# Fused RWKV recurrence and expert layer on one core: zero rows issued ahead of the loads, two copies moved, transposes in the last block, more zero matmuls

## The chip, the core and the metric

One NeuronCore of a Trainium2 chip runs the whole program. The metric is the device time of one execution in microseconds (us), the median of several executions. TensorE is written PE, its weight loads PEld, VectorE DVE, ScalarE ACT, GpSimd Pool; SP is the engine that issues most of the DMAs.

## What is computed

A linear recurrence over 4 batches, 8 heads, 768 tokens and a state of 48 x 48 per head, and then a layer with 8 experts, of which each token uses the one with the highest logit:

```python
for t in range(S):                      # attention part, y is (B, H, S, D)
    cur = np.einsum('bhd,bhe->bhde', u[None] * kt, vt)
    y[:, :, t] = np.einsum('bhd,bhde->bhe', rt, state + cur)
    state = wt[:, :, :, None] * state + np.einsum('bhd,bhe->bhde', kt, vt)
x = y.transpose(0, 2, 1, 3).reshape(B * S, H * D)          # 3072 tokens of 384
logits = x @ w_gate                                        # 8 experts
expert_idx = np.argmax(logits, axis=1)
for e in range(E):
    mask = expert_idx == e
    h = np.maximum(x[mask] @ w1[e], 0.0)                   # 384 -> 1024
    out[mask] = gate_w[mask, None] * (h @ w2[e])           # 1024 -> 384
```

## The kernel before

The recurrence is done in 24 blocks of 64 tokens (two batches to a block, `NB = 24`), one call of `iteration(n)` for each n from -3 to 23. The order of PE, DVE, ACT and Pool is written out by hand: each engine runs its instructions in the order of the Python text, and waits by semaphores for the others.

In `iteration(n)` PE transposes the keys of block n (`pe_kt`, line 474), multiplies by the carried state (`pe_inter`, 442), makes the 64 x 64 scores (`pe_a`, 430), then `pe_xc(n)`: transposes the finished rows of block n-1 (`pe_xT`, 497), makes the bonus coefficients of block n+2 (`pe_c`, 489) and runs some matmuls on zeros whose result nobody reads (`zeros`, 124; 16 of them while n < 4, else 6). Then come `pe_av` (451) and the state update `pe_dp` (463). All of `pe_xc`'s results share one PSUM bank, pool psM, which has one buffer: the next user of psM on PE waits until ACT has copied both the coefficients (`act_ct`, 394) and the transposed rows (`act_xT`, 421) out of it. The next user is, in three blocks of every four, the logits of the previous group of four blocks (`logit_mm` 503, `logit_tr` 510, `rank` 542), else the next block's `pe_xc`.

ACT copies kt out of PSUM (408), writes eight 64 x 64 diagonals of the next block (`act_diag`, 402), the state (`act_g`, 389), then xT, ct, and the finished rows xr (`act_xr`, 416). DVE blends the diagonals with the scores (`dve_at`, 354), which `pe_av` waits for, and does two scans, a reciprocal and a product for later blocks (332, 335, 341, 349). Pool multiplies r by the prefix (`pool_rh`, 376), r by k (`pool_rk`, 368, three blocks ahead; `pe_c` of a later block waits for it), and scatters finished rows by indirect DMA to xs, a table in HBM with 3072 rows per expert (`scatter`, 572), from block 7 on, one block's rows per iteration.

SP's queue issues, in order, the loads of block n+6 (`load`, lines 94 and 97, and `load_v`, 107) in iteration n, each when its buffer (six in a ring) is free. Rows 272 to 463 of each expert in xs are first filled with zero rows from the tile `zrow`, which Pool sets (`zero_rows`, 167, at the end of iteration 0). `prefill(e)` (313) issues the fill for expert e on SP's queue, for e = 0 to 7 at the end of iterations 1 to 8, behind that iteration's loads. Fills and scatters both write xs, so each is held until the ones before it in program order have landed.

From iteration 19 on the experts follow. `choose()` picks the first expert, its weights are loaded in four pieces (`load_piece`, 203 and 206), and `side()` splits one third of a piece into a high and a low part, on ACT (216) and DVE (218). `ua` is the first 256 rows of that expert; `halves(ua)` makes its gate weights (Pool copies gate and row number, 247; DVE adds and inverts, 249 and 250), and `transpose_rows` transposes them (PE 279, ACT 280, DVE 281) into PSUM banks `bk["t"]`. Before the change these banks exist only after `pctx.close()`, which is behind the last block. Then `mm1(ua, f)` (`expand`, 290 to 293) makes 128 of the 1024 hidden features at a time, for f = 0 to 7, between which the last two blocks' logits (`logit_few`, 519), `rank`, `place` and `scatter` stand. `sort_experts()` orders the other experts, SP reads that order into registers (`expert_of`, 651), and their weights are loaded from then on. `contract` (303) and the transposed form at 899 make the second product.

Of the kernel before, what the change touches and what calls it, by code (L numbers as in the profile page):

```python
# [53 lines left out]
def rwkv_moe_kernel(ctx, tc, rkw, vv, ub, wg, wr, w1, w2, out):  # L54
# [11 lines left out]
    psU = pctx.enter_context(tc.tile_pool(name="psU", bufs=1, space=PSUM))  # L66
    psA = pctx.enter_context(tc.tile_pool(name="psA", bufs=1, space=PSUM))
    psY = pctx.enter_context(tc.tile_pool(name="psY", bufs=1, space=PSUM))
    wk = mctx.enter_context(tc.tile_pool(name="wk", bufs=2))
# [59 lines left out]

    pre_ = []  # L130
# [9 lines left out]
    nc.vector.tensor_tensor(out=id2, in0=ident[:, 0:C], in1=ident[:, C:P], op=ALU.add)  # L140
    cmask = acon.tile([P, C], I32, name="cmask")
# [22 lines left out]
    zrow = wst.tile([P, ZJ * XC], F32, name="zrow", tag="wst")  # L164

    def zero_rows():
        nc.gpsimd.memset(zrow, 0.0)
        nc.gpsimd.iota(zrow.bitcast(I32).rearrange("p (j c) -> p j c", c=XC)[:, :, DM + 1], pattern=[[P, ZJ]], base=OOB,
                       channel_multiplier=1)

# [73 lines left out]
    def gate_weights(t):  # L244
        gi = gis.pop()
        p, nq = t.shape[0], t.shape[1]
        nc.gpsimd.tensor_copy(gi.bitcast(I32)[0:p, 0:nq], t.bitcast(I32)[:, :, DM:DM + 2])
        g = gi[0:p, 0:nq, 0:1]
        nc.vector.tensor_scalar(out=g, in0=g, scalar1=1e-9, scalar2=None, op0=ALU.add)
        nc.vector.reciprocal(g, g)  # L250
        return gi[0:p, 0:nq]
# [225 lines left out]
    def pe_xc(n):  # L477
# [3 lines left out]
        zeros(t[:, DM + H:], 16 if n < 4 else 6)  # L481
# [178 lines left out]
    def iteration(n):  # L660
        G, i = divmod(n, GRP)
        g = G - 1 if n >= 0 else -1
        whole = (g, 0, GRP)
        if n >= 0:
# [18 lines left out]
        if n == NB - 1:  # L683
            gate((NG - 1, 0, 2))
            side()
            side()
# [3 lines left out]
        act_diag(n + 1, range(4, 8))  # L690
# [8 lines left out]
        pe_xc(n)  # L699
        dve_pre(n + 2)  # L700
        act_xT(n - 1)
        act_ct(n + 2)
        pe_av(n)
        act_xr(n)
        act_pend(n + 2)
# [13 lines left out]
        if n == 0:  # L719
            zero_rows()  # L720
        if n == 1:
            late_constants()
        if 1 <= n < 9:
            prefill(n - 1)
# [45 lines left out]

    ET = mybir.EngineType
    with tc.manual_schedule(engines={ET.PE, ET.DVE, ET.Activation, ET.Pool}):
        last = NG - 1
        ka, kb = (last, 0, 2), (last, 2, 2)
        for n in range(-3, NB):
            iteration(n)
            if n == FIRST * GRP + 8:
                ua = rows_of(HA, 0, 0)
# [9 lines left out]
        scatter(last - 1, (1, 2, 3))  # L788
        t = psM.tile([P, BANK], F32, name="xc", tag="m")
        pe_xT(NB - 1, t)  # L790
        act_xT(NB - 1)
        pctx.close()
        psN = mctx.enter_context(tc.tile_pool(name="psN", bufs=1, space=PSUM))
        N = [psN.tile([P, BANK], F32, name=f"N{i}") for i in range(6)]
        bk["t"] = N[0:2]
        bk["b"] = [cell] + N[2:4]
        bk["c"] = N[4:6]
        pool_ids(last)
        scatter(last, (0, 1))
# [319 lines left out]
```

## Time and profile before

| | us |
|---|---|
| three executions | 441.26, 440.64, 438.7 |
| median | 440.64 |
| the profiled execution | 436.62 |
| its span, first to last instruction | 434.9 |
| PE busy | 387.4 (89%) |
| PEld busy | 357.4 (82%) |
| DVE busy | 260.1 (60%) |
| ACT busy | 208.8 (48%) |
| Pool busy | 133.2 (31%) |

The mean granted clock of PE over the span is 0.909 of full speed. In a timeline row, the number in brackets is how long the engine had been idle before the instruction, and what released it by the profile; "issue" and "remote" name no instruction of this core. PE's matmuls are pipelined, so the lengths of neighbouring rows overlap, and the start of the next row is the better measure. A wait for several things is put down to the one that came last by the profile, and where the named one had long been done, it was another, often a DMA.

### The profile page before, as it was taken

Reading aid. Unit: us, or ns where it says so; the run is one execution under the profiler, and the core shown is the slowest. Engines: PE = TensorE matmul, PEld = TensorE weight load, DVE = VectorE, ACT = ScalarE, POOL = GpSimd, SP = SyncE. Lnnn points to the kernel's source line nnn. Section 1 sums busy time; section 2 is a strip of 40 time slices with the busy share of each in tenths; the row PEclk is TensorE's granted clock in tenths of the full one; section 3 lists DMA queues with packets and bytes.
Section 4 is the critical chain, followed back from the end, with each engine's and each line's share of the span. In section 5 each row is a group of like instructions: output and inputs, shape, how many; then the busy total and the mean of one; then the engine's idle time right before and its main releaser. Section 6 shows DMA issues by size and latency. Waiting matters only on the chain.

```text
span 434.9 us, 13044 instructions
## 1 busy us (share of the span) xinstructions
PE 387.4 (89%) x5362; PEld 357.4 (82%) x5362; DVE 260.1 (60%) x447; ACT 208.8 (48%) x584; POOL 133.2 (31%) x171
## 2 busy tenths in 40 slices
PE   8879886699888796699889999999999999999890
PEld 6768665588767676599879999999999999999890
DVE  7546788844978764246665646647656577673310
ACT  1545764544667555325455545546456454551200
POOL 3753425573475723310201004004021072104031
PEclk9967999855999977559999999999999999999996
DMA  8996866646563722315955536556555567711001
GB/s 212 247 226 183 210 181 181 183 126 169 167 182 98 235 98 55 130 38 154 333 182 161 182 87 188 189 166 189 184 183 174 153 193 223 229 68 37 16 15 41
DMA packets 38214, 68.10 MB, mean 157 GB/s; under 512 B 8693, under 2 KB 20038, under 8 KB 38147
## 3 DMA queue, kind: packets, MB, share of 16 engines
q1 hardware_dynamic: 31026, 57.68, 46.0%
q0 software_dynamic: 7120, 9.51, 6.8%
q8 instruction: 44, 0.72, 0.7%
q14 instruction: 24, 0.19, 0.1%
HBM read 55.30 MB, written 12.04 MB: 155 GB/s over the span
## 4 chain that ended last, share of the span: by engine, by line
PE 49%; DMA 3%; DVE 2%; issue 1%; ACT 1%; SPq 1%; POOLq 0%; POOL 0%; ACTq 0%
PE N L290 12%; PE N L303 10%; PE N L899 6%; PE cell L290 6%; PE mM L290 5%; PE cell L899 3%; PE mM L899 3%; DMA wst<-in_w_dram 3%; PE N L279 2%; PE N L888 1%; SPq L651 1%; PE lt L519 1%; DVE hl L293 0%; DVE w2l L218 0%; DVE w1l L218 0%
## 5 line engine op out<-in xcount | busy, mean ns | idle before, releaser
L254 POOL DMA_INDIRECT out_dram<-ot,gi x16 | 22.3, 1392 | 103.4 <-issue 72.0
L402 ACT ACTIVATE at<-id,ct 128x64 f32<-128x64 f32 x192 | 50.4, 338 | 0.0
L354 DVE COPY_PREDICATED at<-cmask,ap 128x512 f32<-128x512 int32 x24 | 17.5, 729 | 42.8 <-ACT kt L408 39.0
L376 POOL TENSOR_TENSOR rh<-rkwt,pre 112x512 f32<-112x512 f32 x24 | 28.9, 1204 | 41.5 <-DVE pre L332 33.8
L254 POOL DMA_INDIRECT out_dram<-ort,gi x13 | 17.6, 1356 | 72.6 <-issue 23.6
L572 POOL DMA_INDIRECT xs<-xr,pi x24 | 25.6, 1068 | 44.2 <-issue 12.0
L218 DVE TENSOR_TENSOR w1l<-wst,w1h 128x512 fp32r<-128x512 f32 x48 | 32.9, 690 | 8.4 <-ACT w1h L216 8.2
L303 PE MATMUL N<-w2h,hh 128*126 128x384 f32 (+4 forms) x104 | 36.0, 346 | 1.4 <-ACT hh L292 1.4
L218 DVE TENSOR_TENSOR w2l<-wst,w2h 128x512 fp32r<-128x512 f32 x48 | 32.2, 689 | 6.2 <-ACT w2h L216 5.9
L303 PE MATMUL N<-w2h,hl 128*126 128x384 f32 (+4 forms) x104 | 35.1, 337 | 0.0
L368 POOL TENSOR_TENSOR rk<-rkwt 112x512 f32<-112x512 f32 x24 | 30.6, 1273 | 14.7 <-DMA rkwt<-in_rkw_dram 8.9
L303 PE MATMUL N<-w2l,hh 128*126 128x384 f32 (+4 forms) x104 | 35.0, 337 | 0.0
L293 DVE SCALAR_TENSOR_TENSOR hl<-N,hh 128x256 fp32r<-128x256 f32 (+8 forms) x37 | 19.4, 525 | 25.1 <-ACT hh L292 23.8
L216 ACT ACTIVATE w1h<-wst 128x512 fp32r<-128x512 f32 x48 | 29.6, 623 | 5.2 <-DMA wst<-in_w_dram 5.2
L341 DVE TENSOR_TENSOR_SCAN suf<-rkwt,cell 112x536 f32<-112x536 f32 x24 | 30.5, 1271 | 0.7
L332 DVE TENSOR_TENSOR_SCAN pre<-rkwt,cell 112x536 f32<-112x536 f32 x24 | 30.1, 1255 | 1.3 <-DMA rkwt<-in_rkw_dram 1.3
L216 ACT ACTIVATE w2h<-wst 128x512 fp32r<-128x512 f32 x48 | 28.8, 624 | 4.0 <-DMA wst<-in_w_dram 4.0
L451 PE MATMUL yp<-vt,at 64*64 64x48 f32 x768 | 21.5, 248 | 9.8 <-issue 5.0
L292 ACT ACTIVATE hh<-N 128x256 fp32r<-128x256 f32 (+8 forms) x37 | 17.2, 465 | 26.3 <-PE N L290 25.1
L408 ACT ACTIVATE kt<-ap 128x448 f32<-128x448 f32 x22 | 11.9, 542 | 37.3 <-PE ap L430 33.9
L290 PE MATMUL N<-xh,w1h 128*128 128x440 f32 (+6 forms) x84 | 28.8, 343 | 0.0
L290 PE MATMUL N<-xh,w1l 128*128 128x440 f32 (+6 forms) x84 | 28.6, 341 | 0.0
(182 smaller groups left out, 1027.8 us busy)
## 6 DMA issues: line engine op xcount, KB each, us to landing
wst<-in_w_dram SPq DMA_DIRECT2D x48, 256.0 KB
wst<-in_w_dram SPq DMA_DIRECT2D x16, 768.0 KB
rkwt<-in_rkw_dram SPq DMA_DIRECT2D x72, 96.0 KB
rkwt<-in_rkw_dram SPq DMA_DIRECT2D x24, 238.0 KB
vt<-in_vv_dram SPq DMA_DIRECT2D x24, 192.0 KB
wck_t<-in_wr_dram SPq DMA_DIRECT2D x6, 768.0 KB
rkwt<-in_rkw_dram SPq DMA_DIRECT2D x12, 224.0 KB
xs<-zrow SPq DMA_DIRECT2D x8, 289.5 KB
```

What stands on the lines that cost most here:

```text
L216: nc.scalar.activation(hi, st[:, cs], AF.Copy)
L218: nc.vector.tensor_tensor(out=lo, in0=st[:, cs], in1=hi.bitcast(F32), op=ALU.subtract)
L254: i = nc.gpsimd.indirect_dma_start(out=out[:, :], out_offset=bass.IndirectOffsetOnAxis(ap=t.bitcast(I32)[:, q, 1:2], axis=0), in_=rows, in ...
L290: nc.tensor.matmul(hp, a, x[p][:, j, :], start=(i == 0), stop=(i == 8))
L303: nc.tensor.matmul(op, a[:, cs], w2v(wt, w, f), start=(i == 0), stop=(i == 23))
L332: nc.vector.tensor_tensor_scan(out=d["pt"][:, 0, 0:NW], data0=d["w"], data1=cell[:RP, 0:1].broadcast_to([RP, NW]), initial=1.0, op0=ALU.mu ...
L341: nc.vector.tensor_tensor_scan(out=suf[:, ::-1], data0=d["w"][:, ::-1], data1=cell[:RP, 0:1].broadcast_to([RP, NW]), initial=1.0, op0=ALU. ...
L368: i = nc.gpsimd.tensor_tensor(out=d["rk"], in0=d["r"], in1=d["k"], op=ALU.mult)
L376: nc.gpsimd.tensor_tensor(out=d["rh"], in0=d["r"], in1=d["pre"][:, :, 1:C + 1], op=ALU.mult)
L402: nc.scalar.activation(d["at"][:, h // NQ, h % NQ, :], id2, AF.Copy, scale=d["ct"][:, h:h + 1])
L572: i = nc.gpsimd.indirect_dma_start(out=xsf, out_offset=bass.IndirectOffsetOnAxis(ap=ch["pi", G, b], axis=0), in_=xr[:, b, :], in_offset=No ...
L899: nc.tensor.matmul(pp, w, a, start=(i == 0), stop=(i == 23))
```

## The change

Five edits. (1) The pool with the recurrence's state, psU, gets its own context `uctx` on the right side of PSUM. In block 23 `open_n()` closes it, ahead of the pools of the scores and outputs, and opens two banks for the first rows' transposes; `halves(ua)` and the three calls of `transpose_rows` now stand inside iteration 23 (one of its two calls of `side()` gives way to them), and behind the last block `mm1(ua, 0)` comes ahead of `pe_xT(23)`, the scatters and the remaining logits, so that `mm1(ua, 3)` and no longer `mm1(ua, 2)` is the last ahead of `sort_experts()`. (2) `zero_rows()` runs on Pool during the setup, ahead of the mask, and the eight fills are issued at the head of iterations 0 to 5 (1, 1, 2, 1, 1 and 2 of them), ahead of that iteration's loads. (3) On ACT `act_ct(n+2)` and `act_xT(n-1)` come after four diagonals and the state, two more diagonals ahead of `act_xr(n)` and the last two behind it. (4) `pe_xc` runs 8 zero matmuls in place of 6 for n from 4 to 20, and 14 for n from 21 on. (5) In `gate_weights` DVE reads the gate from the loaded rows, and Pool copies only the row number; `tick()` places its transposes and splits at other points of the first expert's second product.

```diff
--- before.py
+++ after.py
@@ -63,9 +63,10 @@
     psC = mctx.enter_context(tc.tile_pool(name="psC", bufs=1, space=PSUM))
     psM = mctx.enter_context(tc.tile_pool(name="psM", bufs=1, space=PSUM))
     pctx = ExitStack()
-    psU = pctx.enter_context(tc.tile_pool(name="psU", bufs=1, space=PSUM))
     psA = pctx.enter_context(tc.tile_pool(name="psA", bufs=1, space=PSUM))
     psY = pctx.enter_context(tc.tile_pool(name="psY", bufs=1, space=PSUM))
+    uctx = ExitStack()
+    psU = uctx.enter_context(tc.tile_pool(name="psU", bufs=1, space=PSUM, side="right"))
     wk = mctx.enter_context(tc.tile_pool(name="wk", bufs=2))
     WKB = {"suf": 2, "kh": 4, "rh": 4, "rk": 4, "at": 3, "kt": 3, "oT": 2}
 
@@ -127,6 +128,13 @@
     zeros(wrm[:, 0:P], WARM[0])
     zeros(wrm, WARM[1])
 
+    zrow = wst.tile([P, ZJ * XC], F32, name="zrow", tag="wst")
+
+    def zero_rows():
+        nc.gpsimd.memset(zrow, 0.0)
+        nc.gpsimd.iota(zrow.bitcast(I32).rearrange("p (j c) -> p j c", c=XC)[:, :, DM + 1], pattern=[[P, ZJ]], base=OOB,
+                       channel_multiplier=1)
+
     pre_ = []
     for i in range(2):
         t = acon.tile([RP, 2, NW + SEG], F32, name=f"pre{i}")
@@ -138,6 +146,7 @@
     make_identity(nc, ident)
     id2 = const.tile([P, C], F32, name="id2")
     nc.vector.tensor_tensor(out=id2, in0=ident[:, 0:C], in1=ident[:, C:P], op=ALU.add)
+    zero_rows()
     cmask = acon.tile([P, C], I32, name="cmask")
     nc.gpsimd.memset(cmask, -1)
     for i in range(2):
@@ -161,13 +170,6 @@
     flag = const.tile([1, 1], I32, name="flag")
     none = const.tile([1, 1], F32, name="none")
     gis = [const.tile([P, 4, 2], F32, name=f"gi{e}") for e in range(E + 1)]
-    zrow = wst.tile([P, ZJ * XC], F32, name="zrow", tag="wst")
-
-    def zero_rows():
-        nc.gpsimd.memset(zrow, 0.0)
-        nc.gpsimd.iota(zrow.bitcast(I32).rearrange("p (j c) -> p j c", c=XC)[:, :, DM + 1], pattern=[[P, ZJ]], base=OOB,
-                       channel_multiplier=1)
-
     def late_constants():
         nc.gpsimd.memset(tri, 1.0)
         nc.gpsimd.affine_select(out=tri, in_=tri, pattern=[[1, P]], compare_op=ALU.is_gt,
@@ -244,9 +246,9 @@
     def gate_weights(t):
         gi = gis.pop()
         p, nq = t.shape[0], t.shape[1]
-        nc.gpsimd.tensor_copy(gi.bitcast(I32)[0:p, 0:nq], t.bitcast(I32)[:, :, DM:DM + 2])
+        nc.gpsimd.tensor_copy(gi.bitcast(I32)[0:p, 0:nq, 1:2], t.bitcast(I32)[:, :, DM + 1:DM + 2])
         g = gi[0:p, 0:nq, 0:1]
-        nc.vector.tensor_scalar(out=g, in0=g, scalar1=1e-9, scalar2=None, op0=ALU.add)
+        nc.vector.tensor_scalar(out=g, in0=t[:, :, DM:DM + 1], scalar1=1e-9, scalar2=None, op0=ALU.add)
         nc.vector.reciprocal(g, g)
         return gi[0:p, 0:nq]
 
@@ -478,7 +480,7 @@
         t = psM.tile([P, BANK], F32, name="xc", tag="m")
         pe_xT(n - 1, t)
         pe_c(n + 2, t)
-        zeros(t[:, DM + H:], 16 if n < 4 else 6)
+        zeros(t[:, DM + H:], 16 if n < 4 else 8 if n < NB - 3 else 14)
 
     def pe_c(n, t):
         if real(n):
@@ -661,6 +663,9 @@
         G, i = divmod(n, GRP)
         g = G - 1 if n >= 0 else -1
         whole = (g, 0, GRP)
+        if 0 <= n < 6:
+            for e in range(E * n // 6, E * (n + 1) // 6):
+                prefill(e)
         if n >= 0:
             load(n + 6)
             load_v(n + 6)
@@ -683,11 +688,11 @@
         if n == NB - 1:
             gate((NG - 1, 0, 2))
             side()
-            side()
+            open_n()
+            halves(ch["ua"])
         act_kt(n)
         act_diag(n + 1, range(0, 4))
         act_g(n + 1)
-        act_diag(n + 1, range(4, 8))
         dve_at(n)
         if full and i == 3:
             scatter(g, (0, 1) if g == FIRST else (0,))
@@ -697,11 +702,16 @@
             scatter(FIRST, (2, 3))
         pool_rk(n + 3)
         pe_xc(n)
+        if n == NB - 1:
+            for j in range(3):
+                transpose_rows(*(ch["ua"][k] for k in ("t", "nq", "rows", "x")), j)
         dve_pre(n + 2)
+        act_ct(n + 2)
         act_xT(n - 1)
-        act_ct(n + 2)
+        act_diag(n + 1, range(4, 6))
         pe_av(n)
         act_xr(n)
+        act_diag(n + 1, range(6, 8))
         act_pend(n + 2)
         act_pad(n + 4)
         if full and i == 2:
@@ -716,12 +726,8 @@
             t = rank(whole)
             if n == NB - 2:
                 logit_few((NG - 1, 0, 2), t)
-        if n == 0:
-            zero_rows()
         if n == 1:
             late_constants()
-        if 1 <= n < 9:
-            prefill(n - 1)
 
     todo = [(e, i) for e in range(E) for i in range(5) if i < 4 or 0 < e <= NWR]
     out_ = []
@@ -768,6 +774,11 @@
             halves(u)
         transpose_rows(u["t"], u["nq"], u["rows"], u["x"], j)
 
+    def open_n():
+        uctx.close()
+        psT = mctx.enter_context(tc.tile_pool(name="psT", bufs=1, space=PSUM, side="right"))
+        bk["t"] = [psT.tile([P, BANK], F32, name=f"N{i}") for i in range(2)]
+
     ET = mybir.EngineType
     with tc.manual_schedule(engines={ET.PE, ET.DVE, ET.Activation, ET.Pool}):
         last = NG - 1
@@ -775,7 +786,7 @@
         for n in range(-3, NB):
             iteration(n)
             if n == FIRST * GRP + 8:
-                ua = rows_of(HA, 0, 0)
+                ch["ua"] = rows_of(HA, 0, 0)
             if n == NB - 2:
                 for i in range(2):
                     side()
@@ -785,39 +796,38 @@
                 place(ka)
                 for i in range(2):
                     side()
-        scatter(last - 1, (1, 2, 3))
+        ua = ch["ua"]
+        pctx.close()
+        psN = mctx.enter_context(tc.tile_pool(name="psN", bufs=1, space=PSUM))
+        N = [psN.tile([P, BANK], F32, name=f"N{i}") for i in range(2, 6)]
+        bk["b"] = [cell] + N[0:2]
+        bk["c"] = N[2:4]
+
+        def mm1(u, f):
+            expand(wts[u["e"] % 2], f, u["x"], u["n"], u["hs"])
+
+        while sides and sides[0][2] < 2:
+            side()
+        mm1(ua, 0)
         t = psM.tile([P, BANK], F32, name="xc", tag="m")
         pe_xT(NB - 1, t)
         act_xT(NB - 1)
-        pctx.close()
-        psN = mctx.enter_context(tc.tile_pool(name="psN", bufs=1, space=PSUM))
-        N = [psN.tile([P, BANK], F32, name=f"N{i}") for i in range(6)]
-        bk["t"] = N[0:2]
-        bk["b"] = [cell] + N[2:4]
-        bk["c"] = N[4:6]
+        scatter(last - 1, (1, 2, 3))
         pool_ids(last)
         scatter(last, (0, 1))
-        for j in range(3):
-            trans(ua, j)
-
-        def mm1(u, f):
-            expand(wts[u["e"] % 2], f, u["x"], u["n"], u["hs"])
-
-        while sides and sides[0][2] < 2:
-            side()
-        mm1(ua, 0)
+        mm1(ua, 1)
         logit_few(kb)
         gate(kb)
-        mm1(ua, 1)
+        mm1(ua, 2)
         rank(kb)
         weigh(kb)
         place(kb)
         scatter(last, (2, 3))
-        mm1(ua, 2)
+        mm1(ua, 3)
         side(0)
         sort_experts()
         check_counts()
-        for f in range(3, 8):
+        for f in range(4, 8):
             mm1(ua, f)
             side(0)
         actx.close()
@@ -835,9 +845,10 @@
         tr = [(ub_, j) for j in range(3)]
 
         def tick():
-            if tr and nth["k"] % 2:
+            if tr and nth["k"] in ((1, 3, 4) if tr[0][0] is ub_ else (0, 2, 4)):
                 trans(*tr.pop(0))
-            side(nth["e"] + 1)
+            if nth["e"] or nth["k"] > 2:
+                side(nth["e"] + 1)
             nth["k"] += 1
 
         nth["k"] = nth["e"] = 0
```

## Rows read from the trace of the kernel before

**Rows 1.** The page: span, then TensorE's clock and the DMA engines in 40 slices.

```profile
span 434.9 us, 13044 instructions
...
PEclk9967999855999977559999999999999999999996
DMA  8996866646563722315955536556555567711001
```

**Rows 2.** Busy time: stretch, length, PE PEld DVE ACT Pool (instructions), clock, DMA share, GB/s.

```profile
41.70:64.60 22.90, 19.33 (x665) 16.16 (x661) 18.42 (x27) 15.35 (x60) 8.38 (x8) 1.00 0.71 191
64.60:84.30 19.70, 12.58 (x415) 10.22 (x412) 17.10 (x22) 11.80 (x45) 9.98 (x12) 0.96 0.63 171
84.30:105.10 20.80, 20.58 (x431) 17.54 (x431) 10.29 (x14) 9.02 (x33) 13.70 (x17) 0.50 0.52 149
...
177.20:195.40 18.20, 15.21 (x71) 14.53 (x72) 7.47 (x29) 5.31 (x14) 4.81 (x9) 0.50 0.12 45
195.40:223.10 27.70, 25.01 (x180) 24.07 (x179) 17.24 (x37) 14.37 (x33) 2.99 (x4) 1.00 0.74 233
223.10:424.40 201.30, 199.45 (x1155) 195.20 (x1155) 115.89 (x208) 92.53 (x183) 36.81 (x32) 1.00 0.48 146
```

**Rows 3.** Timeline of Pool, 57 to 90 us: start, length, what, idle before.

```profile
65.81 1.20 POOL L572 DMA_INDIRECT xs<-xr,pi  x1 [6.26 <-DMA rkwt<-in_rkw_dram]
...
73.60 1.44 POOL L572 DMA_INDIRECT xs<-xr,pi  x1 [4.12 <-DVE suf L341]
...
81.89 1.01 POOL L572 DMA_INDIRECT xs<-xr,pi  x1 [4.38 <-DVE at L354]
```

**Rows 4.** Timeline of SP's queue, 47 to 92 us: the zero rows.

```profile
60.13 0.48 SPq L313 DMA_DIRECT2D xs<-zrow  x1
...
69.67 0.48 SPq L313 DMA_DIRECT2D xs<-zrow  x1
...
77.95 0.48 SPq L313 DMA_DIRECT2D xs<-zrow  x1
```

**Rows 5.** Timeline of PE, 63 to 90 us.

```profile
84.28 1.03 PE L489 MATMUL xc<-ubt,rk 112*64 112x8 f32 x16 [3.19 <-POOL rk L368]
```

**Rows 6.** PE's waits, 41.7 to 155 us: total, times, longest.

```profile
PE xc L489 <- POOL rk L368: 4.7, 3, 3.2
...
PE lt L510 <- ACT ct L394: 2.1, 3, 0.7
...
PE rank L542 <- ACT ct L394: 1.4, 2, 0.7
PE lp L503 <- ACT ct L394: 1.4, 2, 0.7
```

**Rows 7.** Timeline of ACT in block 13.

```profile
109.31 1.05 ACT L402 ACTIVATE at<-id,ct 128x64 f32<-128x64 f32 x4
```

**Rows 8.** Timeline of PE, the zero matmuls of block 14.

```profile
114.34 0.49 PE L124 MATMUL xc<-wz,ones 128*128 128x120 bf16 x6
```

**Rows 9.** Timeline of PE, 160 to 172 us.

```profile
166.16 0.41 PE L542 MATMUL rank<-base,one 1*128 1x40 f32 x2 [1.38 <-ACT xT L421]
```

**Rows 10.** Timeline of PE, 168 to 196 us: the first rows' transposes.

```profile
177.92 1.06 PE L279 MATMUL N<-ident,xg 128*128 128x128 f32 x4
181.95 0.69 PE L279 MATMUL N<-ident,xg 128*128 128x128 f32 x2 [2.96 <-DVE x L281]
```

**Rows 11.** Timeline of ACT, 163 to 184 us.

```profile
175.14 0.49 ACT L421 ACTIVATE xT<-xc 128x384 f32<-128x384 f32 x1 [4.26 <-remote]
```

**Rows 12.** Timeline of DVE, 163 to 184 us.

```profile
181.20 0.17 DVE L249 TENSOR_SCALAR gi<-gi 128x2 f32<-128x2 f32 x1 [2.39 <-POOL gi L247]
```

**Rows 13.** Chain that ended last, 160 to 235 us: start, length, what.

```profile
207.19 10.23 DMA wst<-in_w_dram
```

**Rows 14.** Timeline of PE, 21 to 28 us.

```profile
25.68 0.99 PE L451 MATMUL yp<-vt,at 64*64 64x48 f32 x27 [2.54 <-issue]
```

**Rows 15.** Busy time by stretch, early.

```profile
20.00:26.00 6.00, 3.46 (x84) 2.84 (x86) 5.61 (x7) 3.47 (x13) 4.30 (x19) 0.89 1.06 240
```

More of the change, by code (lines that the diff above doesn't have):

```diff
@@ L787, in rwkv_moe_kernel @@
                     side()
-        scatter(last - 1, (1, 2, 3))
-        t = psM.tile([P, BANK], F32, name="xc", tag="m")
-        pe_xT(NB - 1, t)
-        act_xT(NB - 1)
+        ua = ch["ua"]
         pctx.close()
         psN = mctx.enter_context(tc.tile_pool(name="psN", bufs=1, space=PSUM))
-        N = [psN.tile([P, BANK], F32, name=f"N{i}") for i in range(6)]
-        bk["t"] = N[0:2]
-        bk["b"] = [cell] + N[2:4]
-        bk["c"] = N[4:6]
-        pool_ids(last)
-        scatter(last, (0, 1))
-        for j in range(3):
-            trans(ua, j)
+        N = [psN.tile([P, BANK], F32, name=f"N{i}") for i in range(2, 6)]
+        bk["b"] = [cell] + N[0:2]
+        bk["c"] = N[2:4]
         def mm1(u, f):
@@ L808, in rwkv_moe_kernel @@
         mm1(ua, 0)
+        t = psM.tile([P, BANK], F32, name="xc", tag="m")
+        pe_xT(NB - 1, t)
+        act_xT(NB - 1)
+        scatter(last - 1, (1, 2, 3))
+        pool_ids(last)
+        scatter(last, (0, 1))
+        mm1(ua, 1)
         logit_few(kb)
         gate(kb)
-        mm1(ua, 1)
+        mm1(ua, 2)
         rank(kb)
```

## The prediction

> **What bounds the kernel now.** First the page: the clock line shows TensorE below full speed in four places, at about 24 to 38, 82 to 106, 150 to 158 and 168 to 195 us [rows 1]. Then busy time by stretch [rows 2]. Behind 223.1 us PE is busy 199.45 of 201.3 us at clock 1.00 and the change touches nothing there: that part moves as a whole, and a gain ahead of it counts in full. Ahead of it the recurrence is uneven. The stretches begin at the first transposes of a block: blocks 4 to 7 take 22.9 us, 5.73 a block, with PE the busiest engine (19.33). Blocks 8 to 12, from 64.6 to 105.1 us, take 40.5 us, 8.1 a block, for the same work, and half of that runs at clock 0.50, the 1.2 GHz level.
>
> Why, Pool and SP's queue side by side show. Pool's first three scatters stand idle 6.26, 4.12 and 4.38 us [rows 3]. The profile names a load, a scan and a blend as releasers, but none of them is an input that comes due then. The times fit a ladder: a fill is issued at 60.13 us, the scatter behind it starts at 65.81; the fill of 69.67 comes 2.7 us after that scatter's row ended (65.81 + 1.20) and the next scatter follows at 73.60; the fill of 77.95, 2.9 us after that one's row (73.60 + 1.44), is followed by the scatter of 81.89 [rows 3, 4]. Fill and scatter both write xs, and each waits until the one before has landed, 3.9 to 5.7 us behind a fill. Pool is in order, so `pool_rk` stands behind each scatter, and PE waits 4.7 us for it in three places, the longest 3.19 us [rows 5, 6]. Behind that longest wait comes the half clock.
>
> **Edit 2, the fills first.** In program order all eight then stand ahead of every scatter, and the last two are issued at the head of iteration 5. The fill of 60.13 us is the one at the end of iteration 6, so that head is two blocks of 5.73 us sooner, at about 49 us; the first scatter's turn is at 65.81 - 6.26 = 59.6 us. Against 3.9 to 5.7 us of landing the wait is gone, and the two fills that queue behind scatters no longer hold up the loads behind them on SP. What is late next is PE itself. Five blocks at 5.73 us are 28.6 us against 40.5: **-11.9 us**. `zero_rows` on Pool moves to the setup, where PE, DVE and Pool wait for the first load anyway: nothing, and at most its own 1 us or so if that cover were gone. The fills now share the queue with the loads of blocks 6 to 11, each ahead of one: the loads run six blocks ahead, over 30 us, and eight fills of 290 KB at the 240 GB/s of [rows 15] are 1.2 us each. I take 0 for it; what it might cost is a rival.
>
> **Edit 3, ct and xT ahead of half the diagonals.** In seven blocks between 41.7 and 155 us PE waits 0.71 us at the user of psM behind `pe_dp`, 2.1 + 1.4 + 1.4 = 4.9 us in all, put down to ct, the last of the two copies [rows 6]. Four diagonals take 1.05 us on ACT [rows 7], and these move behind the copies: 0.71 goes wholly, and PE is late by its own work next. In blocks 8 to 12, four more such users, 2.8 us. Two diagonals stay ahead of `act_xr`, two go behind it: that copy too comes some 0.5 us sooner, and the late diagonals have most of a block before `dve_at` wants them. **Edit 4, more zeros.** Six take 0.49 us [rows 8], 0.08 each at most, so two more cost 0.16 us a block, 2.8 us over 17 blocks, if nothing hides them. So edits 3 and 4 together: between -4.9 us and nothing, since DVE is busy 18.42 us of the same 22.9 as PE [rows 2], and where a blend waits for DVE the freed time turns into a wait for it. I take **-3**.
>
> **Last blocks, 21 to 23.** Eight more zeros in each of three blocks are at 0.08 us 1.9 us. Against them stand block 21's wait of 0.71 and most of the 1.38 us that `rank` waits for xT in block 22 [rows 9], 1.05 of it by the diagonals. Sum: **+0.2**, between -1.8 (the zeros fill waits) and +1.
>
> **Edits 1 and 5, the transposes.** Now they stand between the last block and the first expert: from 177.92 us to the first product at about 182.6, 4.7 us, of which PE waits 2.96 [rows 10], because DVE waits 2.39 us for Pool's copy of the gates, which is behind scatters [rows 12]. In block 23 the six transposes take 1.06 + 0.69 us at the half clock, beside a wait of PE for DVE's blend; I count 0.3. Added: `mm1(ua, 0)` now wants the fifth split part of w1, which is made behind the last `rank`. A wait that the trace doesn't show; from about 1 us to as much as the 2.96 that it replaces; I take 1.5 below, since ACT is also copying there. Also one more product, `mm1(ua, 3)`, goes ahead of the sort. At 177.2 to 195.4 us, clock 0.50, PE ran 71 matmuls in 15.21 us busy [rows 2], 0.21 each, so nine are 1.9 us; `pe_xT(23)` only changes places with `mm1(ua, 0)`. -4.7 + 0.3 + 1.5 + 1.9 = **-1.0**, between -3.5 and +1.5.
>
> The sort matters because the second expert's weights are loaded by it, and the chain that ended last runs through 10.23 us of one such load [rows 13], with DMA at 0.74 of its engines' time in 195.4 to 223.1 us [rows 2]. An earlier end of PE's queue alone would be worth less.
>
> **Sum.** -11.9 - 3 + 0.2 - 1.0 = -15.7 us. The profiled execution took 436.62 us, span 434.9 and 1.7 around it, 4.0 less than the median of 440.64. I take the gain off the median: **424.9 us** (420.9 for an execution like the profiled one). With the terms' bounds added up (-4.9 to 0, -1.8 to +1, -3.5 to +1.5) it lies between 418.5 and 431.2, before the cases below.
>
> **Rivals.**
> *The clock holds into the experts.* The half clock from 168 us on follows idle stretches of PE in blocks 22 and 23: 1.38 us [rows 9], then more while ACT stands still 4.26 us with no releaser [rows 11]. With 14 zeros and the transposes in there the clock may stay at 2.4 GHz. Then 177.2 to 195.4 us with 15.21 us of matmuls gives back some 7 us, block 23 another 1: 417. For it speaks that the 1.38 us goes; against it, that nothing in the change removes the 4.26. Chance 0.30.
> *The early DMA traffic bites.* At 20 to 26 us the DMA engines are busy 1.06 of their time [rows 15], and there PE stands 2.54 us in the middle of one product, released by nothing shown [rows 14]; half clock follows [rows 1]. Eight fills in place of four by the head of iteration 5 lengthen the full stretch. One more such stop, 2.5 us, and two blocks at the half clock behind it: at 0.50, 431 matmuls took 20.8 us, 8.0 us for a block's 166, against 5.73 [rows 2]: 2.5 + 2 x 2.3 = 7 us, 432. Chance 0.15.
> The Trainium skill ("Runtime: NRT & Kernel Launch", section Instruction fetch mechanics) has each engine's instructions streamed over a DMA queue of their own, block by block, with the cost of crossing a block mostly hidden. If PE's stop is such a crossing, by that rule this rival would cost nothing and the forecast would stand; the 2.54 us row doesn't look hidden, and no row here shows that it is a fetch.
> *It doesn't do what it says.* If the scatters wait for the load that the profile names [rows 3] and not for a fill, the -11.9 stays away and 436.8 is left, faster by 0.9%. The ladder speaks against it. Chance 0.05.
> *Slower.* The DMA engines stay full until the fills are through, and PE stops in each of blocks 1 to 6 as in block 1: 2.5 + 2.3 us each, 29 us, against 15.7 gained: 454. It decides from 3.3 such blocks on (15.7 / 4.8). Against it: at 41.7 to 64.6 us, with four fills in it, the DMA share was 0.71 and the clock 1.00 [rows 2]. Chance 0.05.
>
> **Chances.** Forecast 0.45, own range 418.5 to 431; clock holds 0.30; one early stop 0.15; no effect of the fills 0.05; slower 0.05. The range reaches down to the held clock with half of the upside of the terms (414) and up to one early stop (433), and leaves out the last two cases and the far tails. About 0.5% (2.2 us) is what a measurement of this kernel can tell from no change. Faster by more than that: the forecast, the held clock, the early stop and most of the fourth case, 0.92; within it 0.04; slower 0.04.
>
> **What would show it.** Right: Pool's first scatter starts without a wait of several us, no PE wait for `pool_rk`, clock 1.00 from 41 to beyond 105 us, block 13 beginning near 90 us in place of 105.1; no 0.71 us waits for ct; all transposes of `ua` ahead of the last block's `pe_av`. Wrong: a scatter idle for 4 us still, half clock in blocks 3 to 8, DVE ending most of PE's waits, or a gap of over 2 us of PE ahead of `mm1(ua, 0)`. The sum would fail most easily at the tail, where the clock decides, and at blocks 4 to 20, if they run well below 5.73 us.

## Result, and the profile of the changed kernel

Beside the kernel before on one chip the changed kernel took **421.44 us** (median of 415.95, 420.69, 422.19 and 423.52) against 439.67 (436.52 to 441.26): a ratio of 0.955, 95% interval 0.944 to 0.967. The forecast was 424.9, range 414 to 433. Two repeats in later groups, told below, gave 418.3 against 435.8 and 418.1 against 430.2, the second with a ratio of 0.970 (0.963 to 0.977). So the changed kernel nearly keeps its time (418 to 421 us), and the kernel before moves: the gain is 12 to 18 us. The ratios here and below leave out executions more than 1.5% above the fastest of the same kernel, while medians and ranges hold them all.

The profiled execution is the slowest of the four: 423.52 us, its span 421.8, the mean granted clock 0.936. From its page, to be laid beside [rows 1]:

```profile
span 421.8 us, 13190 instructions
PE 383.2 (91%) x5419; PEld 353.2 (84%) x5420; DVE 257.0 (61%) x447; ACT 208.1 (49%) x584; POOL 133.7 (32%) x171
...
PEclk9997888998999595699999999999999999999996
DMA  8998855575662714128974456375466557801001
```

Of the half clock that [rows 1] show at 82 to 106 us a dip at 94 to 98 is left; the one at 30 to 36 us stands in both, and two are new, at 50 to 54 and 60 to 67 us. Busy time by stretch, as in [rows 2] (blocks 4 to 7, blocks 8 to 12, from `rank(ka)` on, the experts):

```profile
core 0: us, PE busy (x) PEld busy (x) DVE busy (x) ACT busy (x) POOL busy (x), PEclk, DMA share, GB/s
40.60:66.90 26.30, 23.43 (x674) 20.12 (x668) 19.15 (x28) 16.47 (x63) 11.73 (x12) 0.81 0.68 183
66.90:97.70 30.80, 27.15 (x854) 22.82 (x851) 24.14 (x34) 19.66 (x76) 19.21 (x23) 0.94 0.60 172
169.70:185.00 15.30, 15.21 (x103) 14.37 (x100) 8.42 (x30) 8.00 (x20) 4.66 (x8) 0.78 0.14 53
208.20:411.30 203.10, 199.76 (x1158) 195.26 (x1158) 117.40 (x210) 93.64 (x186) 37.83 (x33) 1.00 0.50 149
```

Blocks 8 to 12 take 30.8 us in place of 40.5, but blocks 4 to 7 take 26.3 in place of 22.9, at clock 0.81. The experts' stretch, begun here one matmul later than in [rows 2], takes 203.1 us in place of 201.3. Pool's first scatters, which stood 6.26, 4.12 and 4.38 us in [rows 3] (start, duration, idle before it and releaser):

```profile
62.17 1.20 POOL L574 DMA_INDIRECT xs<-xr,pi  x1 [3.39 <-DMA vt<-in_vv_dram]
...
67.47 1.01 POOL L574 DMA_INDIRECT xs<-xr,pi  x1 [0.16 <-ACT rkwt L382]
...
73.36 1.01 POOL L574 DMA_INDIRECT xs<-xr,pi  x1 [0.15 <-ACT ls L508]
```

The ladder is gone (the first still waits 3.39 us, at a half-clock block). PE's waits between 41 and 155 us, the view of [rows 6] (what waited, for what: us in all, times, longest):

```profile
PE ap L432 <- issue: 4.5, 7, 1.3
PE U L465 <- issue: 3.4, 3, 1.7
PE yp L453 <- DVE at L356: 1.3, 2, 0.9
PE yp L444 <- ACT xr L418: 1.0, 3, 0.4
```

No wait for rk (4.7 before) and 0.5 for ct (4.9 before). In their place stands "issue": time in which PE waited for nothing that the profile shows. What that is turned out to be the main question of the experiments.

### The profile page after: what moved, and what is told of

Same layout as the page of the kernel before. It is cut to its first block, busy times and chain, and to the rows that moved or that the text cites. A ratio compares the mean times of both kernels' runs of the same rounds, so it can differ in the third digit from the quotient of the medians.

```text
span 421.8 us, 13190 instructions
## 1 busy us (share of the span) xinstructions
PE 383.2 (91%) x5419; PEld 353.2 (84%) x5420; DVE 257.0 (61%) x447; ACT 208.1 (49%) x584; POOL 133.7 (32%) x171
## 4 chain that ended last, share of the span: by engine, by line
PE 73%; DVE 9%; issue 6%; DMA 4%; ACT 4%; another core or an unknown queue 1%; SPq 1%; POOLq 0%; POOL 0%; DVEq 0%; ACTq 0%
PE N L292 11%; PE N L305 10%; PE cell L292 6%; PE N L910 6%; PE mM L292 5%; PE yp L453 3%; PE xc L125 3%; PE cell L910 3%; DMA wst<-in_w_dram 3%; PE mM L910 3%; PE ap L432 3%; PE xc L491 2%; PE yp L444 2%; PE wrm L125 2%; PE U L465 2%
## 5 line engine op out<-in xcount | busy, mean ns | idle before, releaser
L256 POOL DMA_INDIRECT out_dram<-ot,gi x16 | 22.3, 1392 | 100.4 <-issue 72.0
L404 ACT ACTIVATE at<-id,ct 128x64 f32<-128x64 f32 x192 | 53.3, 343 | 0.0
L295 DVE SCALAR_TENSOR_TENSOR hl<-N,hh 128x256 fp32r<-128x256 f32 (+8 forms) x37 | 19.4, 524 | 24.1 <-ACT hh L294 22.8
L294 ACT ACTIVATE hh<-N 128x256 fp32r<-128x256 f32 (+8 forms) x37 | 17.2, 465 | 24.3 <-PE N L292 23.1
L410 ACT ACTIVATE kt<-ap 128x448 f32<-128x448 f32 x22 | 11.9, 543 | 34.9 <-PE ap L432 31.2
L292 PE MATMUL N<-xh,w1l 128*128 128x440 f32 (+6 forms) x84 | 28.6, 341 | 0.0
L292 PE MATMUL N<-xl,w1h 128*128 128x440 f32 (+6 forms) x84 | 28.6, 340 | 0.0
```

The lines of the kernel that those rows point to most:

```text
L256: i = nc.gpsimd.indirect_dma_start(out=out[:, :], out_offset=bass.IndirectOffsetOnAxis(ap=t.bitcast(I32)[:, q, 1:2], axis=0), in_=rows, in ...
L292: nc.tensor.matmul(hp, a, x[p][:, j, :], start=(i == 0), stop=(i == 8))
L404: nc.scalar.activation(d["at"][:, h // NQ, h % NQ, :], id2, AF.Copy, scale=d["ct"][:, h:h + 1])
```

## Experiments

Each kernel's diff is against the kernel named; " ..." marks lines left out. The kernels stood in three groups of four, each group on one chip beside the kernel before, whose medians there were 431.8 (the single edits), 435.8 (the four after that) and 430.2 us (the last four).

**The fills alone** (before, with edit 2).

```diff
+    zero_rows()
 ...
+        if 0 <= n < 6:
+            for e in range(E * n // 6, E * (n + 1) // 6):
+                prefill(e)
 ...
-        if n == 0:
-            zero_rows()
 ...
-        if 1 <= n < 9:
-            prefill(n - 1)
```

> The kernel before with edit 2 alone: zero rows set in the setup, eight fills at the head of iterations 0 to 5. Theory 1, each late fill holds the scatter behind it until it has landed and with it pool_rk and PE: 9 to 12 us faster (ratio 0.973 to 0.980), blocks 8 to 12 in 29 to 31 us in place of 40.5, no PE wait for pool_rk, scatters idle under 0.5 us from block 8 on. Theory 2, the stretch is slow for want of PE work at the blend (the copies, edit 3) and the fills only coincide with it: under 3 us faster, a scatter still idle for over 2 us. Theory 3, the early traffic costs PE stops in blocks 0 to 7: blocks 4 to 7 take 25 us or more in place of 22.9, as the profile of the changed kernel has it (26.3), and the gain is 6 to 9 us.

Measured: 427.5 us against 431.8, ratio 0.982 (0.971 to 0.993), so 4 us and not 9 to 12. Theory 1's mechanism is there (no PE wait for rk, the second to fourth scatter idle 0.16 us at most, blocks 8 to 12 in 31.9 us), and so is theory 3's loss: blocks 4 to 7 take 27.5 us, at clock 0.73. The gain is below what either theory gave.

**Copies and eight zeros alone** (before, with edit 3 and 8 zeros).

```diff
-        zeros(t[:, DM + H:], 16 if n < 4 else 6)
+        zeros(t[:, DM + H:], 16 if n < 4 else 8)
 ...
-        act_diag(n + 1, range(4, 8))
 ...
-        act_xT(n - 1)
         act_ct(n + 2)
+        act_xT(n - 1)
+        act_diag(n + 1, range(4, 6))
         pe_av(n)
         act_xr(n)
+        act_diag(n + 1, range(6, 8))
```

> The kernel before with edit 3 (ct and xT ahead of half the diagonals) and 8 zero matmuls in place of 6 from block 4 on, no other edit. Theory 1, the 0.71 us waits for ct go and DVE's blend takes part of it back: 3 us faster, between 0 and 4.9, PE waits for ct under 1 us in all in place of 4.9. Theory 2, the blend now waits for the two diagonals that moved: the waits move from ct to DVE's blend, time within 1 us of before. Theory 3, the two zeros lie in the open: 1 to 3 us slower.

Measured: 431.5 against 431.8, ratio 0.9995 (0.995 to 1.004): nothing. All PE waits for ct are gone between 41 and 155 us, yet the same view shows:

```profile
PE xc L489 <- POOL rk L368: 5.9, 3, 3.9
PE ap L430 <- issue: 5.9, 4, 3.6
PE U L463 <- issue: 3.5, 3, 1.9
PE yp L451 <- DVE at L354: 2.4, 3, 1.2
```

The blend did not take the time back (2.4 us, 3.0 before), as theory 2 wanted. In this profile the waits with no releaser did (11.1 us in the whole view, 4.0 before). That the edits call them forth isn't shown: 3.57 us of the 11.1 are one stop at 151.6 us, and the fills alone and the tail alone, without these edits, have its like (3.34 us at 148.2, 3.21 at 150.0).

**The tail alone** (before, with edits 1 and 5 and 14 zeros in blocks 21 to 23).

```diff
-        zeros(t[:, DM + H:], 16 if n < 4 else 6)
+        zeros(t[:, DM + H:], 16 if n < 4 else 6 if n < NB - 3 else 14)
 ...
-            side()
+            open_n()
+            halves(ch["ua"])
 ...
+        if n == NB - 1:
+            for j in range(3):
+                transpose_rows(*(ch["ua"][k] for k in ("t", "nq", "rows", "x")), j)
 ...
         mm1(ua, 0)
+        t = psM.tile([P, BANK], F32, name="xc", tag="m")
+        pe_xT(NB - 1, t)
+        act_xT(NB - 1)
+        scatter(last - 1, (1, 2, 3))
```

> The kernel before with edits 1 and 5 (the first rows transposed in block 23, gates without Pool's copy, mm1(ua, 0) ahead of the last copies) and 14 zero matmuls in blocks 21 to 23, fills and copies as before. Theory 1, a path shortened by the transposes, with the clock as it was: 1 us faster, between 3.5 faster and 1.5 slower; rank(ka) to the order's being ready 17 to 18.4 us. Theory 2, with the transposes out of the gap PE goes on without a stop and the clock returns earlier: 5 to 9 us faster, rank(ka) to the order ready in 13 to 14 us in place of 18.4, full clock from about 8 us behind rank(ka) on.

Measured: 427.3 us (421.6 to 432.0) against 431.8; the spread of its four executions leaves no interval. The trace is plainer. The 7 us behind `rank(ka)` by busy time, first of before, then of this kernel, and two of this kernel's PE rows:

```profile
176.00:183.00 7.00, 3.57 (x18) 3.03 (x18) 2.62 (x8) 3.19 (x8) 2.69 (x5) 0.50 0.25 94
```
```profile
172.50:179.50 7.00, 6.13 (x49) 5.55 (x49) 3.79 (x12) 3.60 (x11) 2.55 (x4) 1.00 0.33 128
```
```profile
175.25 0.39 PE L291 MATMUL cell<-x,w1l 128*128 128x256 f32 x1 [0.31 <-DVE w1l L219]
...
179.35 0.40 PE L543 MATMUL rank<-base,one 1*128 1x24 f32 x2
```

49 matmuls in place of 18, at 2.4 GHz in place of 1.2; `rank(kb)` starts 6.8 us behind `rank(ka)` (172.58) in place of 13.0. That is theory 2 by its mechanism; the 4.5 us of the medians lie just under the 5 to 9 that it gave.

**The changed kernel with late fills** (edit 2 undone).

> The changed kernel with edit 2 undone: zero rows and fills as before (iterations 0 and 1 to 8), all other edits in. Theory 1, the fills carry most of the gain: 8 to 12 us slower than the changed kernel, 429 to 433 us; scatters idle 4 to 6 us again in blocks 7 to 9, blocks 4 to 7 back to 23 us. Theory 2, the other edits carry it: within 4 us of the changed kernel's 421.4. If the edits' gains add up, this run and the one with the fills alone sum to the whole gain of 18 us.

Measured: 426.1 us against before's 431.8, ratio 0.985 (0.975 to 0.996). The changed kernel was not in this group; against its 418 to 421 us elsewhere it is 5 to 8 slower, between the two theories. Blocks 4 to 7 are back at 22.0 us, blocks 8 to 12 take 34.1. The 5.6 us won here and the 4.2 of the fills alone come to some 10 us, not to the 18 of the first comparison.

**The changed kernel again.**

> The changed kernel itself, beside the kernel before on the chip of the single edits' sort of clock. The edits measured one by one (fills alone 4.2 us, copies and 8 zeros 0.3, tail alone 4.5) add up to 9.0 us, against 18.2 in the first comparison. Theory 1, the edits add up, and the first comparison caught the kernel before on a chip where it ran slow: 2 to 2.5% faster than before here. Theory 2, they help one another (a wait taken out keeps the clock up for the next edit): 3.5 to 4.5% faster.

Measured: 418.3 us (410.8 to 423.4) against 435.8 (427.5 to 437.6). Before's seven executions here lie in two groups, at 427.5 to 428.6 and at 435.8 to 437.6, so 17.5 us is an upper end; the medians of its three short executions and of the changed kernel's two (410.8 and 416.9) lie 14 us apart, and theory 1 is not refuted. But this profile has one of the longest stops without a releaser, 3.34 us in the middle of one product, and the packet that goes with it (a PE row; then the line of the DMA queues for 142.9 to 143.0 us):

```profile
141.45 0.41 PE L432 MATMUL ap<-rh,kh 64*64 64x64 f32 x13
145.20 0.91 PE L432 MATMUL ap<-rh,kh 64*64 64x64 f32 x19 [3.34 <-issue]
```
```profile
q8 instruction: 1, 0.02, 58.5%
```

A packet of 0.02 MB on the instruction queue starts when PE has already stood for 1 us; by the packet's own times it lands at 143.86, and PE goes on 1.34 us behind that. Ahead of it SP's queue had asked for 2.3 MB of weights:

```profile
133.21 4.04 SPq L205 DMA_DIRECT2D wst<-in_w_dram  x6
137.44 0.39 SPq L208 DMA_DIRECT2D wst<-in_w_dram  x1
```

**The weight pieces one per block.**

```diff
-            feed()
+            feed(1)
+        if FIRST * GRP + 8 <= n < FIRST * GRP + 10:
+            feed(n - FIRST * GRP - 6)
 ...
-    def feed():
-        while len(out_) < 3:
+    def feed(most=3):
+        while len(out_) < most:
```

> The changed kernel with the first expert's first three weight pieces (768 KB each) asked for one per block, in blocks 19, 20 and 21, and not all three in block 19. In the profiles of before, of the changed kernel and of the four single edits PE stands, or its results come, 2 to 3.6 us late in block 20 or 21, about 1.3 us behind the landing of a 16 KB packet of the instruction queue that had started behind this load. Theory 1, PE's next instructions wait in the DMA engines behind bulk data: no stop of over 1.5 us in blocks 20 and 21, full clock there, 3 to 5 us faster than the changed kernel of the same call. Theory 2, the stop belongs to what PE, ACT or Pool do in these blocks: it stays at 2 to 3.6 us, time the same.

Measured: 414.6 us against the changed kernel's 418.3 in the same group, so 3.7 less, with ranges that overlap (408.4 to 418.4; 410.8 to 423.4). The stop of 3.34 us is now one of 1.49, and from 133 to 150 us the clock stands at half for 3.4 us only (PE; then the page's clock):

```profile
136.61 0.61 PE L453 MATMUL yp<-vt,at 64*64 64x48 f32 x19 [1.49 <-issue]
```
```profile
PEclk9959999999999898999999999999999999999996
```

The stop followed the load and not the block: theory 1, in this trace. The other profiles bear it out in part. Behind 133 us six of the ten with the pieces asked for at once have a stop of 2.7 to 3.6 us; of the four with spread pieces, those told below among them, none has one over 2.11, but each has one of 1.49 or more. Its 408.4 us is the shortest of the profiled executions.

**Six zeros** (the changed kernel, edit 4 undone: `zeros(..., 16 if n < 4 else 6)`).

> The changed kernel with edit 4 undone: 6 zero matmuls from block 4 on, also in blocks 21 to 23, and not 8 and 14. Theory 1, the zeros fill waits and cost nothing, and do nothing for the clock either: within 1 us of the changed kernel of the same call. Theory 2, they lie in the open: 2.8 + 1.9 us by the prediction's own prices, so 3 to 5 us faster than the changed kernel. Theory 3, they hold the clock: 2 to 5 us slower, half clock in more of the 40 slices between block 4 and the experts.

Measured: 415.5 us against 418.3, ranges overlapping (408.1 to 417.6). A gain of the size of theory 2 can't be told from chance here; see the second run of this kind below.

**All fills behind the setup's loads.**

```diff
-        if 0 <= n < 6:
-            for e in range(E * n // 6, E * (n + 1) // 6):
+        if n == -1:
+            for e in range(E):
                 prefill(e)
```

> The changed kernel with all eight fills issued right behind the loads of the setup, and not over the first six blocks. Theory 1, PE's stops with no releaser in blocks 2 to 7 of the changed kernel (1.95, 1.09 and 1.73 us) come from its instructions queueing behind fills and loads: stops of 30 to 60 us down to one at most, more of them before 30 us, blocks 4 to 7 near 23 us in place of 26.3, 2 to 4 us faster than the changed kernel of the same call. Theory 2, the loads alone make them: the same stops in blocks 2 to 7, time within 1 us. Theory 3, the loads of block 6 on come late behind the fills: a wait for a load at block 6 or 7, slower.

Measured: 414.7 us (414.5 to 423.0) against 418.3. Blocks 4 to 7 take 21.5 us, where the changed kernel took 28.3 in this group. Stops remain (1.31 us at 42 us, 0.74 at 50), three are now ahead of 32 us (2.43, 0.90 and 2.22), and no PE wait for a load shows. Theory 1 for the blocks; the count of stops is not what it said.

**Both together; the spread weights with late fills; both with six zeros; the changed kernel a third time.** The diffs are those above, put together.

> The changed kernel with both: the first expert's weight pieces asked for one per block, and all fills right behind the setup's loads. Theory 1, both take bulk data out of the way of PE's instructions and each keeps some of its gain: 408 to 413 us, 2 to 3% faster than the changed kernel of the same call, no stop of over 1.5 us behind 35 us. Theory 2, what is measured between kernels is chance in where PE happens to stop: within 3 us of the changed kernel of the same call, and stops of other lengths in other places.

> The changed kernel with the weight pieces one per block, and with edit 2 undone (fills at the ends of iterations 1 to 8, zero rows set at the end of iteration 0). It measures edit 2 without the long stop of blocks 20 and 21. Theory 1, waits for fills in blocks 7 to 9 cost what Pool and PE stand, but the prediction's 11.9 us was mostly a half clock that came with them by chance: 4 to 6 us slower than the same kernel with the fills in iterations 0 to 5 (414.6 us). Theory 2, the prediction's size: 10 to 12 us slower. Theory 3, early fills cost as much in blocks 1 to 7 as late ones in 7 to 9: within 2 us.

> The kernel with weight pieces one per block and fills behind the setup's loads, with 6 zero matmuls in place of 8 and 14. Theory 1, the zeros lie in waits: within 1.5 us of the same kernel with them. Theory 2, they cost their own time now that the stops are fewer: 2 to 4 us faster. Theory 3, they hold the clock: 2 to 5 us slower.

> The changed kernel, in the same call as the versions above and the kernel before, so that all stand on one chip. If the single edits add up: 2.5 to 3.5% faster than before; if the first comparison's size holds: 4 to 4.5%.

| kernel | median, us | range | ratio to before (430.2) |
|---|---|---|---|
| changed, third time | 418.1 | 413.6 to 423.4 | 0.970 (0.963 to 0.977) |
| spread weights, fills first | 416.5 | 406.8 to 420.0 | 0.954 (0.945 to 0.963) |
| the same, six zeros | 416.6 | 414.9 to 420.7 | 0.974 (0.968 to 0.980) |
| spread weights, fills late | 420.7 | 416.1 to 425.5 | 0.983 (0.977 to 0.989) |

The ratios and the medians order the kernels differently, and the second row's ratio rests on two executions (406.8 and 411.3). The changed kernel's third run is 2.8 to 3.0% faster than before, what its expectation has for edits that add up. The version with both beats it by 1.6 us in the median; whether that is real stays open. Its expected 408 to 413 was missed, and stops of 1.79 and 1.70 us remain behind 138 us. By the medians the zeros make no difference (416.6 and 416.5), theory 1, and late fills cost 4.2 us, theory 1 too, though measured against fills behind the setup's loads and not against the kernel that the expectation names. By the ratios late fills cost between 4 and 13 us. The kernel with late fills shows the price of the ladder without half-clock blocks ahead of it: blocks 4 to 7 run at clock 1.00 in 22.3 us, and then come the scatters, PE's waits and the busy time of blocks 8 to 12:

```profile
63.55 1.20 POOL L573 DMA_INDIRECT xs<-xr,pi  x1 [4.53 <-DMA rkwt<-in_rkw_dram]
...
71.17 1.01 POOL L573 DMA_INDIRECT xs<-xr,pi  x1 [3.94 <-DVE suf L342]
...
80.21 1.01 POOL L573 DMA_INDIRECT xs<-xr,pi  x1 [5.57 <-DVE pre L333]
```
```profile
PE xc L490 <- POOL rk L369: 6.2, 3, 4.6
```
```profile
64.30:99.70 35.40, 27.98 (x870) 23.58 (x865) 26.78 (x34) 20.32 (x75) 21.66 (x26) 0.86 0.60 179
```

35.4 us for blocks 8 to 12, against 29.0 at clock 1.00 with the fills first (the same view of that kernel):

```profile
44.50:66.20 21.70, 19.57 (x680) 16.56 (x676) 18.16 (x28) 15.43 (x59) 10.46 (x11) 1.00 0.58 168
66.20:95.20 29.00, 25.48 (x869) 21.38 (x862) 23.78 (x34) 19.69 (x74) 20.21 (x25) 1.00 0.65 197
```

The two lie 6.4 us apart, and PE's waits for rk are 6.2. PE is busy 2.5 us longer there (clock 0.86) and idle 3.9 us longer, so the waits for rk stand in part where the other kernel idles for other reasons. The ladder itself, which the prediction read from times of issue alone, shows here in the landings: the scatter of 63.55 us lands at 67.22 and the next fill is issued at 67.24; that of 71.17 lands at 75.41, and the next fill is issued at 75.42. Each waits for the one before.

## Why the forecast held, and which of its terms did not

Executions of one kernel differ by up to 13 us, so the terms are better read from all fourteen profiles by stage: the start of the first score product (`ap<-rh,kh`) of a block, and PE's last instruction. The a(n) below are those starts. Means, in us:

| | 0 to a(13) | a(4) to a(8) | a(8) to a(13) | a(13) to a(23) | a(23) to the end |
|---|---|---|---|---|---|
| late fills (5 profiles) | 102.6 | 23.1 | 36.2 | | |
| fills in iterations 0 to 5 (6) | 98.2 | 26.6 | 29.3 | | |
| fills behind the setup's loads (3) | 94.1 | 21.7 | 29.2 | | |
| copies as before (3) | | | | 63.1 | |
| copies moved, weights at once (7) | | | | 61.4 | |
| copies moved, weights spread (4) | | | | 59.1 | |
| tail as before (3) | | | | | 253.6 |
| new tail (11) | | | | | 247.6 |

The stages' differences add up to -4.4 - 1.7 - 6.0 = -12.1 us, what the last group measured (418.1 - 430.2). The forecast's terms were -11.9, -3, +0.2 and -1.0. Some of the prediction's own signs failed: half clock in blocks 4 to 7, which it had called a sign of being wrong, stood at 50 to 54 and 60 to 67 us; the first scatter still waited 3.39 us; block 13 began at 97.7 us and not near 90.

*Edit 2, -11.9.* The mechanism is right: the ladder of fills and scatters, the wait for rk behind it, and that PE is next (28.6 us forecast for blocks 8 to 12, 29.3 measured). The term is mis-sized at its other end and at its cover. 40.5 us was one profiled execution; five profiles with late fills take 33.4 to 40.7. The waits come to 6.2 us in the kernel with spread weights and late fills, and its stretch is 6.4 us longer. Half clock comes with them in blocks 8 to 12 of all five, for 10 to 14 us in four and for 23.9 in the one trace that the forecast used; with early fills it is 0 to 9 us. In the means the stretch shrinks by 36.2 - 29.3 = 6.9. And "I take 0 for it" on the queue was wrong: the early fills cost 26.6 - 23.1 = 3.5 us in blocks 4 to 7, which is the rival of the early traffic at half its price of 7. PE's stops of 0.5 us or more there are one to three in ten of these eleven profiles, of either kind. What differs is the clock behind them: five of the six profiles with fills in iterations 0 to 5 have 10 to 17 us of half clock in these blocks and take 26.3 us or more, and so does one of the five with late fills (6.8 us, 25.9); the other eight profiles have none and take 21.5 to 23.1. Net -4.4.

*Edits 3 and 4, -3.* The waits of 0.71 us went wholly, as forecast. At full clock something is left of it: blocks 4 to 7 take 23.1 us in before's profile, the only one of that kind with the old copies, and 21.5 to 23.1 us, in the mean 22.1, in the seven with the moved ones. But the edits alone gave 0.3 us, between 2.1 faster and 1.6 slower, and the -1.7 of the table lies within the spread of its profiles (62.4 to 64.1 with the old copies, 58.6 to 65.2 with the moved ones). What the forecast named as next (PE's own work, or DVE's blend) didn't take the rest; in the profile of the edits alone, stops with no releaser stand in its place, and why they do is open. The zeros, bounded at 2.8 us, cost nothing that two pairs of kernels can show.

*Tail, +0.2 and -1.0.* Mis-sized the other way: 6.0 us. Most steps are right one by one: the 2.96 us wait of [rows 10] is 0.6 to 0.9 us in ten of the eleven profiles (for the changed kernel's own see below); the new wait for the fifth split part is there, at 0.31 us behind 0.48 us for its ACT half with the tail alone; the six transposes stand in block 23. The step that failed is the clock, which the sum held at 0.50 and left to a rival with 0.30. In the three profiles with the old tail the half clock lasts until 17 to 20 us behind `rank(ka)` (the fourth dip of [rows 1] is one); in ten of the eleven with the new one it ends between 10 us ahead of and 7 us behind `rank(ka)`, in the eleventh 15 us behind. In the changed kernel's own profile it ends at 176.5 us, 6.8 behind, where before it ended at 195.4, 19.4 behind. So what stands ahead of the sort, the added product too, runs at twice the clock that the sum took. The zeros aren't needed for it: in the two kernels with six of them in blocks 21 to 23 the half clock ends 6.5 and 6.7 us behind `rank(ka)`.

A second step failed, "the change touches nothing there" of what lies behind 223.1 us. From one and the same matmul of the first expert's second product (at 223.95 us in before, 208.64 in the changed kernel) to PE's last one, the three profiles with the old tail take 200.4 to 200.5 us; of the eleven with the new one none takes less than 202.7, six take 202.7 to 202.9, and the mean is 203.6. So the new tail gains 9 us ahead of that point and loses 3 behind it. Two waits that before doesn't have stand there in all eleven (0.90 and 0.6 us), in the changed kernel:

```profile
214.67 0.50 PE L281 MATMUL N<-ident,xg 110*128 110x110 f32 x3 [0.90 <-DVE xl L283]
```
```profile
243.37 0.54 PE L899 MATMUL N<-ident,oT 128*110 128x128 f32 x3 [0.60 <-ACT oT L917]
```

They follow `tick()`'s new places for transposes and splits; no run has `tick()` changed by itself, so that it alone makes them isn't shown.

*The baseline.* 15.7 us were taken off 440.64, a median of three executions. Over the four groups before's median was 430.2 to 439.7 us, and over the three that hold the changed kernel the gain was 12.1 to 18.2. That the total came out near is in good part luck: the terms erred in both directions, and the start was taken from the group in which before was slowest. (The range's upper end of 433 is 1 us above what the early stop's own sum gives, 424.9 + 7.)

*Not explained.* In the changed kernel's block 23 ACT stands 5.86 us at the first copy of the transposed rows (161.30 to 167.16), as it stood 4.26 in [rows 11], and PE waits behind it:

```profile
168.06 0.69 PE L281 MATMUL N<-ident,xg 128*128 128x128 f32 x2 [3.33 <-DVE x L283]
```

PE's transposes begin at 163.66 us, so that copy comes 3.5 us behind them; in the other thirteen profiles, two of the same kernel among them, it comes 0.6 to 0.8 us behind. No instruction packet is near. It is left open. So is the price of the fills' traffic alone: a kernel without any fill wasn't tried, since it would read rows that nothing wrote.

## What to carry over

Price a wait by the wait and not by the length of the stretch that has it: the half clock that comes with it differs from execution to execution (10 to 24 us here), and further profiles show by how much. When a stall goes, look at what is queued in the DMA engines at that time, since PE's own instructions come through them; spread bulk loads or put them where PE has slack. A short PE gap at the border of two phases can be worth more than its length, when the clock stays down for what follows: here a wait of 2.96 us, and 6.0 us for the stage. And compare also the stretch that the change is taken to leave alone.

## What the runs showed of the hardware

By all that these traces show, PE's stops with no releaser are waits for its own instructions. The page of the changed kernel lists a queue of instructions (packets, MB, share of 16 engines):

```profile
q8 instruction: 44, 0.72, 0.8%
```

Each packet has 0.72 MB / 44, some 16 KB. PE's 10839 matmuls and weight loads are some 250 to a packet, and the packets come as PE uses them up: about every 5 us in the recurrence, every 20 to 25 us in the experts' long products, so the queue is taken to be PE's. Over all fourteen profiles, between 15 and 165 us, there are 108 PE stops of 0.5 us or more without a releaser; 107 of them end 1.15 to 1.67 us behind the landing of such a packet. And they go by the traffic: in the 3 us ahead of a packet the DMA engines' busy share was 0.75 or more for 203 packets, of which 81 were followed by a stop; 0.4 to 0.75 for 145, with 25; under 0.4 for 86, with one. One of these stops in the changed kernel (the packet of 27.48 us lands at 28.42; the queue's line is that of 27.4 to 27.6 us, the PE row the stop that follows):

```profile
q1 hardware_dynamic: 17, 0.06, 116.3%
q8 instruction: 1, 0.02, 29.3%
```
```profile
29.75 0.47 PE L432 MATMUL ap<-rh,kh 64*64 64x64 f32 x3 [1.95 <-issue]
```

The Trainium skill ("Runtime: NRT & Kernel Launch", section Instruction fetch mechanics) has an engine fetch blocks of 16 KiB, 256 instructions, over a DMA queue of its own; the packets agree with that. The Trainium skill, in the same section, calls the cost of crossing a block mostly hidden. With little DMA traffic the traces agree (1 stop in 86 packets); with much of it they don't (81 in 203, up to 3.6 us), and the measurement decides. The prediction's own sentence on the 2.54 us row left open whether it was a fetch: a packet of 16 KB lands at 24.08 us in that trace, 1.60 ahead of the row's start at 25.68.

The two clock levels (2.4 and 1.2 GHz) then make executions of the same code differ. In the third run of the changed kernel the mean clock was 0.914 and the span 421.7 us, in its second run 0.941 and 415.1; the kernel with the weight pieces spread had 0.970 and 406.6. Half clock stands behind stops of PE in all of them, but not behind each.
